# Nystrom attention and a multiplicative FFN on one core: the opening reordered, the second batch's attention moved, the iterated inverse on eight tiles

## The chip, the cores and the metric

The kernel runs on one core of one Trainium2 chip. A core has five engines: TensorE (PE in the profile; its weight loads are PEld), VectorE (DVE), ScalarE (ACT), GpSimd (POOL) and SyncE (SP). Each works through its own queue in order and they wait for one another by semaphores. Transfers are issued from the queues of SP, ACT and POOL and carried out by 16 DMA engines. Matmul results go to PSUM, everything else lives in SBUF.

The metric is the device time of one execution in microseconds. The profile is one execution taken by the hardware profiler; its span runs from the first to the last instruction.

## The reference

The inputs are q, k and v of 8 batches, 8 heads, 576 positions and 64 columns, and four weights. Everything is FP32 in and out.

```python
q_lm = q.reshape(B, H, m, S // m, D).mean(axis=3)      # m = 32 landmarks of 18 rows
k_lm = k.reshape(B, H, m, S // m, D).mean(axis=3)
A  = sm(q, k_lm);  Bm = sm(q_lm, k_lm);  C = sm(q_lm, k)     # softmax of scaled products
Z = Bm.transpose(0, 1, 3, 2) / (norm1(Bm) * norminf(Bm) + 1e-06)
for _ in range(6):
    Z = 2 * Z - Z @ Bm @ Z
x = A @ Z @ C @ v                                      # heads put side by side: 4608 x 512
a = x @ w1;  b = x @ w2                                # 512 x 1024 each
out = (a * b) @ w3 @ w_out                             # 1024 x 1024, 1024 x 512
```

`Z` is an inverse of the 32 x 32 matrix `Bm` by iteration, one for each batch and head.

## The kernel before, in words

**Fold.** `w3 @ w_out` doesn't depend on the tokens, so it is multiplied out once into `w34` (1024 x 512, FP16). For precision both factors are split into a high and a low FP16 half and three of the four cross products are summed. `turn(j, cc)` transposes half a row block of w3 on PE (four FP32 transposes into a `big` PSUM buffer, L453), ACT copies the high half out (L458) and DVE makes the low half (L459). `split_wout` does the same to w_out in four pieces on DVE (L444, L446). A fold step is the three matmuls of 512 columns for one j and one c (L488); there are 8 row blocks j of 8 steps c, so 64 steps. When a row block is done, ACT copies it out (L491).

**Attention.** `attention` is a generator that a batch passes through in 18 steps: the landmarks' matmul (L162) and `lm`; `Bm` (L178); the scores of C (L203) in two steps; scores of A (L253) in two; C @ v (L281, L286) in two; six steps of the inverse (L344); two that normalise A (L329), and four blocks of `g` (L390), the last of the two being in one step with the first block. `g` is `Z C v` times w1 or w2, in blocks of 128 x 1024. The eight heads of a batch lie as 4 x 2: head h of four on partitions 32h to 32h+31, and qd in 0, 1 on the columns.

In the inverse, `sz_` holds 96 columns per qd: 32 of the matrix that is squared (the identity is added to it) and 64 of the vectors that it is applied to. One iteration multiplies the 32 x 32 matrix with all 96 columns, on the four diagonal 32 x 32 tiles of the array, qd by qd; DVE copies the new matrix (L350) and adds the 64 columns to the old ones (L351). The last iteration leaves the matrix out.

**Before attention.** `load_qk` fetches k and q of a batch with a cast to FP16, on POOL's queue. `transposes` turns them by DMA transposes on SP's queue (L89), four to a batch. `landmarks` sums groups of 18 rows and splits the sum in two FP16 halves on POOL, in six instructions each for k and q (L145 to L154).

**Up and down.** For each batch `up(st, j, w)` multiplies A's normalised scores with a 128-column block of g (L404): w = 0 gives a, copied out by ACT (L408), w = 1 gives b, and DVE multiplies both into `ab` (L410). `down` multiplies `ab` with `w34` (L424) for 128 rows at a time in two halves; ACT copies out (L430) and SP stores.

**Order.** The program is written in the order in which it is issued, and each engine keeps it: there is no planner. While batch b goes through `up` and `down`, batch b + 2's loads and landmarks and batch b + 1's attention are woven in by `steps`. The first batch's attention is woven into the fold. PSUM has eight banks: three `big` buffers of two banks, one `small`, one `acc`. SBUF pools have two buffers for most tiles; w3 blocks have three, w_out has one whole tile.

The opening of the program, before:

```python
        nc.gpsimd.tensor_copy(out=gate, in_=wof[:, 2, 0:1])    # holds q and k back until w_out's 2nd piece
        load_qk(sts[0], 0)
        load_w3(2)
        ...
        steps(fd, 5)
        load_w3(3)
        turn_all(0)
        load_v(sts[0], 0)
        steps(fd, 8)
```

Of the kernel before, what the change touches and what calls it, by code (L numbers as in the profile page):

```python
# [14 lines left out]
H = 8  # L15
# [16 lines left out]
def kernel(  # L32
# [52 lines left out]
    def transposes(st, t, hs):  # L85
        if "qkT" not in st:
# [6 lines left out]

    ident = consts.tile([128, 128], FP32, name="ident")
    nc.gpsimd.memset(ident, 0.0)
    nc.gpsimd.affine_select(out=ident, in_=ident, compare_op=ALU.not_equal, fill=1.0,
                            base=0, pattern=[[-1, 128]], channel_multiplier=1)

    def constants():

        mask4 = consts.tile([128, 4, 32], FP32, name="mask4")
        par = consts.tile([128, 2], FP32, name="par")
        ones = consts.tile([128, 1], FP32, name="ones")
        eye = consts.tile([128, 2, 32], FP32, name="eye")
        iit = consts.tile([128, 2, 64], FP16, name="iit")
        onesq = consts.tile([128, 2, 4, 2, 4], FP16, name="onesq")
        nc.vector.memset(mask4, 0.0)
        nc.vector.memset(par, 0.0)
        nc.vector.memset(ones, 1.0)
        nc.vector.memset(onesq, 0.0)  # L110
        for i in range(2):
            sl = slice(64 * i, 64 * i + 64)
            nc.vector.memset(par[sl, i:i + 1], 1.0)
            for jj in range(2):
                nc.vector.tensor_copy(out=iit[sl, jj, :], in_=ident[sl, sl])
        for h in range(4):
            sl = slice(32 * h, 32 * h + 32)
            nc.vector.memset(mask4[sl, h, :], 1.0)
            for qd in range(2):
                nc.vector.tensor_copy(out=eye[sl, qd, :], in_=ident[sl, sl])  # L120
                nc.vector.memset(onesq[sl, qd, :, qd, h:h + 1], 1.0 / X64)

        selc = consts.tile([128, 2, 4, 128], FP16, name="selc")
        lomask = consts.tile([128, 1], FP32, name="lomask")
        selr = consts.tile([128, 8], FP32, name="selr")
        nc.vector.memset(selc, 0.0)
        nc.vector.tensor_tensor(out=selr, in0=eye[:, 0, 0:8], in1=eye[:, 0, 8:16], op=ALU.add)
        nc.vector.reduce_sum(out=lomask, in_=eye[:, 0, 8:16], axis=AX.X)
        nc.vector.tensor_scalar(out=lomask, in0=lomask, scalar1=-1.0, scalar2=None, op0=ALU.mult)
        for c in range(4):  # L130
            sl = slice(32 * c, 32 * c + 32)
            for qd in range(2):
                nc.vector.tensor_copy(
                    out=selc[sl, qd, c, :].rearrange("p (h m) -> p h m", m=32),
                    in_=selr[sl, 4 * qd:4 * qd + 4].unsqueeze(2).to_broadcast([32, 4, 32]),
                )
        return mask4, par, ones, eye, iit, onesq, selc, lomask


    def landmarks(st, t):  # L140
        if "parts" not in st:
            st["parts"] = pz.tile([128, 2, 2, H, 32], FP16, name="parts")
        x = st["qkT"][:, t, :, :, :]
        tr = pat.tile([128, H, NP], FP32, name="tr", bufs=1)
        nc.gpsimd.tensor_tensor(out=tr, in0=x[:, :, 0, :], in1=x[:, :, 1, :], op=ALU.add)  # L145
        nc.gpsimd.tensor_tensor(out=tr, in0=tr, in1=x[:, :, 2, :], op=ALU.add)  # L146
        t3 = tr.rearrange("p h (l g) -> p h l g", g=3)
        o = pat.tile([128, H, 32], FP32, name="o3", bufs=1)
        hi, lo = st["parts"][:, 0, t, :, :], st["parts"][:, 1, t, :, :]
        nc.gpsimd.tensor_tensor(out=o, in0=t3[:, :, :, 0], in1=t3[:, :, :, 1], op=ALU.add)  # L150
        nc.gpsimd.tensor_tensor(out=o, in0=o, in1=t3[:, :, :, 2], op=ALU.add)  # L151

        nc.gpsimd.tensor_copy(out=hi, in_=o)
        nc.gpsimd.tensor_tensor(out=lo, in0=o, in1=hi, op=ALU.subtract)  # L154


    def attention(st, bank=None):
# [111 lines left out]
        sz_ = pz.tile([128, 2, 96], FP32, name="sz_")  # L269
        for qd in range(2):  # L270
            nc.vector.scalar_tensor_tensor(
                out=sz_[:, qd, 0:32], in0=psR[:, 32 * qd:32 * qd + 32], scalar=nrn[:, qd:qd + 1],
                in1=eye[:, qd, :], op0=ALU.mult, op1=ALU.add)
# [63 lines left out]
        for it in range(6):  # L337
            last = it == 5
            psI = small()
            o = 32 if last else 0  # L340
            for qd in range(2):
                for h in range(4):
                    sl = slice(32 * h, 32 * h + 32)
                    nc.tensor.matmul(psI[sl, 96 * qd + o:96 * qd + 96], sz_[sl, qd, 0:32],  # L344
                                     sz_[sl, qd, o:96], start=True, stop=True,
                                     tile_position=(32 * h, 32 * h))
            pv_ = psI[:, 0:192].rearrange("p (a m) -> p a m", m=96)
            if not last:
                nsz = pz.tile([128, 2, 96], FP32, name="sz_")
                nc.vector.tensor_copy(out=nsz[:, :, 0:32], in_=pv_[:, :, 0:32])  # L350
                nc.vector.tensor_tensor(out=nsz[:, :, 32:96], in0=sz_[:, :, 32:96],  # L351
                                        in1=pv_[:, :, 32:96], op=ALU.add)
                sz_ = nsz
            else:
                xd = pz.tile([128, 2, 64], FP32, name="xd")
                nc.vector.tensor_tensor(out=xd, in0=sz_[:, :, 32:96], in1=pv_[:, :, 32:96],
                                        op=ALU.add)
# [84 lines left out]
    def split_wout(wof, c0):  # L442
        sl = slice(c0, c0 + 2)
        nc.vector.tensor_scalar(out=wsp[:, 0, sl, :], in0=wof[:, sl, :], scalar1=WS, scalar2=None,  # L444
                                op0=ALU.mult)
        nc.vector.scalar_tensor_tensor(out=wsp[:, 1, sl, :], in0=wof[:, sl, :], scalar=WS,  # L446
                                       in1=wsp[:, 0, sl, :], op0=ALU.mult, op1=ALU.subtract)

    def fold(pf, wof, w3f):
        def turn(j, cc):  # L450
# [5 lines left out]
            w3t = pf.tile([128, 2, 4, 128], FP16, name="w3t")  # L456
# [4 lines left out]
            return w3t  # L461


        blocks = [(0, 0), (1, 0), (0, 1), (1, 1)] + [(j, cc) for j in range(2, 8) for cc in range(2)]
        turned, psW = {}, {}

        def turn_next(n):
            if n < 16:
                turned[blocks[n]] = turn(*blocks[n])

        turn_next(0)
        split_wout(wof, 0)
        for n, (j, cc) in enumerate(blocks):
            if cc == 0:
                psW[j] = small() if j in (1, 3) else acc()
            for c4 in range(4):
                c = 4 * cc + c4

                if n < 4 and c4 == 1:
                    turn_next(n + 1)  # L480
                    if n < 3:
                        split_wout(wof, 2 * n + 2)
                elif n >= 4 and cc == 0 and c4 == 0:
                    turn_next(n + 1)
                elif n >= 4 and cc == 1 and c4 == 1:
                    turn_next(n + 1)
                for a, b in ((0, 0), (0, 1), (1, 0)):
                    nc.tensor.matmul(psW[j][:, :], turned[j, cc][:, a, c4, :], wsp[:, b, c, :],  # L488
                                     start=(c == 0 and a + b == 0), stop=(c == 7 and a == 1))
                if c == 7:  # L490
                    nc.scalar.activation(out=w34[:, j, :], in_=psW[j][:, :], func=AXF.Copy,  # L491
                                         scale=1.0 / (WS * WS))
                yield
# [14 lines left out]
    with tc.tile_pool(name="pf", bufs=2) as pf:  # L508
        wof, w3f = pf.tile([128, 8, DM], FP32, name="wof", bufs=1), {}
# [8 lines left out]
        for j, cc in ((0, 0), (1, 0), (0, 1), (1, 1)):  # L518
            load_w3(j, cc)
        for c in range(0, 8, 2):  # L520
            nc.scalar.dma_start(
                out=wof[:, c:c + 2, :],
                in_=moe_w_out[128 * c:128 * c + 256, :].rearrange("(c p) f -> p c f", p=128))
# [4 lines left out]
        for _ in range(8):  # L528
            nc.tensor.matmul(psw[:, 0, :], warm[:, 0:128], warm, start=True, stop=True)

        nc.gpsimd.tensor_copy(out=gate, in_=wof[:, 2, 0:1])
        load_qk(sts[0], 0)
        load_w3(2)
        mask4, par, ones, eye, iit, onesq, selc, lomask = constants()
        fd = fold(pf, wof, w3f)
        steps(fd, 5)
        load_w3(3)
        turn_all(0)
        load_v(sts[0], 0)
        steps(fd, 8)  # L540
        load_w3(4)
        landmarks(sts[0], 1)
        load_weight(0, moe_w1)
        landmarks(sts[0], 0)
        load_weight(1, moe_w2)
        load_qk(sts[1], 1)
        steps(fd, 8)
        load_w3(5)
        steps(fd, 8)
        load_w3(6)  # L550
        steps(fd, 6)
        at = attention(sts[0])
        for n in range(28):
            steps(at)
            if n == 4:
# [3 lines left out]
            if n == 10:  # L559
                landmarks(sts[1], 1)  # L560
                landmarks(sts[1], 0)
                load_qk(sts[2], 2)
            steps(fd)
        steps(at, 30)
        steps(fd, 64)
    pab = ctx.enter_context(tc.tile_pool(name="pab", bufs=3))
    at = attention(sts[1], acc)
    steps(at)


    for b in range(B):
# [10 lines left out]
        for j in range(8):  # L582
            up(st, j, 0)
            steps(at)
# [46 lines left out]
```

## Time and profile before

| | |
|---|---|
| median of 5 runs | 304.4 us (301.79 to 305.02) |
| the profiled execution | 305.99 us, span 304.2 us |
| PE busy | 281.4 us, 93% of the span |
| DVE, POOL, ACT busy | 162.8, 147.0, 121.6 us |
| first matmul of the fold | 9.42 us |
| the sixteen steps of row blocks 0 and 1 done | 31.40 us |
| the second batch's landmark matmul, first up after it | 85.12 us, 85.55 us |
| from there to the third batch's landmark matmul | 27.76 us |

A page shows one execution. Its first part gives the busy time of each engine; the second cuts the span in 40 slices, with a digit for the busy tenths of each engine in each slice, the clock granted to PE in tenths (PEclk), and the busy share of the DMA engines. A timeline gives groups of instructions in order of time: start, duration, engine, line, operation, out<-in, partitions and shape, count, and in brackets how long the engine was idle before and what ended that. Matmul ends are modelled, so the distance between starts of groups is the better measure of what a group holds PE.

### The profile page before, as it was taken

What the parts mean: (1) busy time and instruction counts of PE and PEld (TensorE: products, weight loads), DVE (VectorE), ACT (ScalarE), POOL (GpSimd) and SP (SyncE); (2) the same over time, 40 slices, a digit from 0 to 9 for tenths busy, and PEclk for the clock granted to TensorE, in tenths of its full rate; (3) what the DMA queues carried; (4) which work ended last, traced back from release to release, by engine and by line L of the source; (5) the groups of instructions that cost most, each with busy time, mean ns of one, the idle gap of its engine ahead of it and who ended that gap; (6) DMA issues with size and microseconds to landing.
All of it is one profiled execution on the core that took longest, in us unless ns stands there. A gap on an engine that the chain in (4) does not pass through costs nothing.

```text
span 304.2 us, 9351 instructions
## 1 busy us (share of the span) xinstructions
PE 281.4 (93%) x3976; PEld 154.8 (51%) x3976; DVE 162.8 (54%) x411; ACT 121.6 (40%) x197; POOL 147.0 (48%) x187
## 2 busy tenths in 40 slices
PE   5586999599999999999999999999999999999994
PEld 2233555343566437643764674367447544754641
DVE  6533224246355657664665765476566556666620
ACT  1102235104255257235733752474167235624532
POOL 0205964109629925980796299239907930600000
PEclk9579999989999999999999999999999999999998
DMA  7989999992299939993999599389959632003114
GB/s 230 327 158 190 274 225 250 213 134 42 33 208 210 207 83 167 193 211 91 149 210 226 123 203 213 99 115 163 246 152 168 134 104 74 2 18 90 38 45 127
DMA packets 66121, 46.74 MB, mean 154 GB/s; under 512 B 39712, under 2 KB 58144, under 8 KB 66080
## 3 DMA queue, kind: packets, MB, share of 16 engines
q1 hardware_dynamic: 51360, 32.52, 50.0%
q0 software_dynamic: 13632, 11.54, 24.4%
q10 hardware_dynamic: 1088, 2.10, 1.9%
q8 instruction: 31, 0.51, 0.7%
q14 instruction: 10, 0.08, 0.1%
HBM read 38.80 MB, written 9.44 MB: 159 GB/s over the span
## 4 chain that ended last, share of the span: by engine, by line
PE 85%; ACT 6%; DVE 4%; issue 2%; DMA 2%; ACTq 0%
PE big L404 20%; PE acc L424 12%; PE acc L488 11%; PE big L424 10%; PE small L344 7%; PE big L390 6%; PE small L488 3%; PE small L281 2%; ACT a_sb L408 2%; PE big L453 2%; PE acc L281 2%; DMA wof<-in_moe_w_out_dram 2%; DVE wsp L446 2%; PE big L329 2%; PE big L203 2%
## 5 line engine op out<-in xcount | busy, mean ns | idle before, releaser
L404 PE MATMUL big<-ahat,gt 128*128 128x288 f16 x512 | 74.5, 287 | 2.2 <-ACT a_sb L408 1.6
L410 DVE TENSOR_TENSOR ab<-a_sb,big 128x576 f16<-128x576 f16 x64 | 48.0, 751 | 18.1 <-PE big L404 10.8
L408 ACT CAST a_sb<-big 128x576 f16<-128x576 f32 x64 | 40.9, 639 | 39.1 <-PE big L404 38.4
L404 PEld LDWEIGHTS <-gt 128*128 128x128 f16 x512 | 46.1, 98 | 18.7 <-issue 4.4
L214 POOL TENSOR_TENSOR t<-ect 96x384 f32<-96x384 f32 x16 | 15.9, 995 | 71.6 <-ACT ect L207 71.1
L488 PE MATMUL acc<-wsp,w3t 128*128 128x512 f16 x144 | 39.8, 405 | 9.3 <-DVE wsp L444 5.9
L424 PE MATMUL acc<-w,ab 128*128 128x512 f16 (+1 forms) x192 | 40.9, 382 | 0.0
L145 POOL TENSOR_TENSOR tr<-qkT 128x768 f32<-128x768 f16 x16 | 27.2, 1702 | 28.0 <-DMA qkT<-qkn 28.0
L424 PEld LDWEIGHTS <-ab 128*128 128x128 f16 (+1 forms) x320 | 24.1, 100 | 32.2 <-issue 9.7
L488 PEld LDWEIGHTS <-w3t 128*128 128x128 f16 x192 | 18.3, 101 | 31.6 <-issue 14.2
L424 PE MATMUL big<-w,ab 128*128 128x512 f16 x128 | 32.8, 382 | 0.0
L396 DVE TENSOR_SCALAR gt<-big 128x1024 f16<-128x1024 f32 x16 | 19.6, 1225 | 20.2 <-PE big L390 20.2
L459 DVE SCALAR_TENSOR_TENSOR w3t<-big,w3t 128x512 f16<-128x512 f32 x16 | 11.1, 692 | 29.7 <-ACT w3t L458 29.6
L146 POOL TENSOR_TENSOR tr<-tr,qkT 128x768 f32<-128x768 f32 x16 | 26.3, 1641 | 1.3
L430 ACT ACTIVATE o_sb<-acc 128x512 f32<-128x512 f32 x20 | 11.9, 597 | 36.1 <-PE acc L424 35.1
L458 ACT ACTIVATE w3t<-big 128x512 f16<-128x512 f32 x16 | 9.5, 595 | 35.7 <-PE big L453 35.7
L394 ACT ACTIVATE gt<-big 128x1024 f16<-128x1024 f32 x16 | 16.4, 1024 | 7.9 <-PE big L390 7.9
L390 PE MATMUL big<-wup,zt 64*32 64x512 f16 x512 | 19.2, 381 | 0.0
L430 ACT ACTIVATE o_sb<-big 128x512 f32<-128x512 f32 x16 | 9.6, 597 | 23.3 <-PE big L424 23.3
L207 ACT ACTIVATE ect<-big 96x768 f32<-96x768 f32 x16 | 12.9, 806 | 2.3 <-PE big L203 1.9
L151 POOL TENSOR_TENSOR o<-o,tr 128x256 f32<-128x256 f32 x16 | 12.8, 800 | 1.3
L332 DVE TENSOR_TENSOR ahat<-eat,big 128x576 f16<-128x576 f16 x16 | 12.0, 748 | 1.4 <-PE big L329 1.4
(298 smaller groups left out, 354.5 us busy)
## 6 DMA issues: line engine op xcount, KB each, us to landing
vt<-in_v_dram SPq DMA_DIRECT2D x8, 1152.0 KB, 9.3
qkn<-in_k_dram POOLq DMA_DIRECT2D x8, 576.0 KB, 9.7
qkn<-in_q_dram POOLq DMA_DIRECT2D x8, 576.0 KB, 12.7
out_dram<-o_sb SPq DMA_DIRECT2D x24, 192.0 KB, 2.3
w3f<-in_moe_w_dram SPq DMA_DIRECT2D x6, 512.0 KB, 8.2
out_dram<-o_sb SPq DMA_DIRECT2D x24, 128.0 KB, 3.1
wof<-in_moe_w_out_dram ACTq DMA_DIRECT2D x4, 512.0 KB, 8.3
wup<-in_moe_w_dram POOLq DMA_DIRECT2D x4, 512.0 KB, 10.6
```

The lines of the kernel that those rows point to most:

```text
L145: nc.gpsimd.tensor_tensor(out=tr, in0=x[:, :, 0, :], in1=x[:, :, 1, :], op=ALU.add)
L146: nc.gpsimd.tensor_tensor(out=tr, in0=tr, in1=x[:, :, 2, :], op=ALU.add)
L344: nc.tensor.matmul(psI[sl, 96 * qd + o:96 * qd + 96], sz_[sl, qd, 0:32], sz_[sl, qd, o:96], start=True, stop=True, tile_position=(32 * h, ...
L390: nc.tensor.matmul(psG[32 * h:32 * h + 32, qd, :], zt[rs, i, h, :], wup[rs, h, w, fs], start=(i == 0), stop=(i == 1), tile_position=(64 * ...
L394: nc.scalar.activation(out=g[:, :, w, fs], in_=psG, func=AXF.Copy, scale=1.0 / ZS)
L396: nc.vector.tensor_scalar(out=g[:, :, w, fs], in0=psG, scalar1=1.0 / ZS, scalar2=None, op0=ALU.mult)
L404: nc.tensor.matmul(p[:, c, 0:HS], st["g"][:, qd, w, 128 * j:128 * j + 128], st["ahat"][qd][:, c, :], start=(qd == 0), stop=(qd == 1))
L408: nc.scalar.copy(out=st["a_sb"], in_=p[:, :, 0:HS])
L410: nc.vector.tensor_tensor(out=st["ab"][:, j, :].rearrange("p (c s) -> p c s", c=2), in0=st["a_sb"], in1=p[:, :, 0:HS], op=ALU.mult)
L424: nc.tensor.matmul(pso[o:o + sz, :], ab[:, j, s0:s0 + sz], w34[:, j, :], start=(j == 0), stop=(j == 7), tile_position=(0, o))
L430: nc.scalar.activation(out=o_sb, in_=pso[:, :], func=AXF.Copy, scale=1.0 / (X64 * X64))
L488: nc.tensor.matmul(psW[j][:, :], turned[j, cc][:, a, c4, :], wsp[:, b, c, :], start=(c == 0 and a + b == 0), stop=(c == 7 and a == 1))
```

## The change

**q and k of the first batch on PE.** `turn_on_pe` makes 12 transposes of 96 x 128 FP16 blocks into a `big` buffer, for four heads of k or q, and ACT or DVE copies them to `qkT`. Four calls take the place of the four DMA transposes of this batch. The first batch's landmarks of k stay on POOL, those of q go to DVE, in two halves.

**Fold.** w_out is held in pieces of 256 rows, three buffers; three are loaded by ACT's queue, the fourth by SP's once the first is split. The order of steps weaves row blocks 0 and 1 by piece: both take the two steps of piece 0, then both of piece 1, and so on. w3's transposed halves have four buffers. Warm-up matmuls are ten instead of eight.

**Loads.** w1 and w2 are issued right behind the first batch's q and k; v moves ahead of w3 blocks 3 and 4; the second batch's q and k come earlier. The first batch's attention starts after 24 fold steps (35 before), with two fold steps between its steps instead of one.

**Second batch's attention.** It no longer starts ahead of the first batch's `up`, but after j = 2, and takes 0, 0, 0, 1, 1, 1, 2, 2 steps in the eight j. Its k landmarks come after the fold on POOL, its q landmarks on DVE at j = 1.

**Inverse.** The matrix of the product is kept apart with 2I added (`tz_`), so that the product gives the new 96 columns outright. The order is h outside, qd inside, and qd = 1 goes to the tile beside the diagonal (`t = h ^ qd`): eight tiles with one product each. The two heads' places swap at each of the six iterations. The result goes to a `big` buffer, one bank for each qd.

```diff
+    def turn_on_pe(st, t, h0, copy):
+        if "qkT" not in st:
+            st["qkT"] = pat.tile([128, 2, H, 3, NP], FP16, name="qkT")
+        ps = psp.tile([128, 2, 1024], FP16, name="big", bufs=3)
+        for i in range(2):
+            for n in range(6):
+                nc.tensor.transpose(
+                    out=ps[:, i, NP * n:NP * n + NP],
+                    in_=st["qkn"][0:NP, t, h0 + 2 * i + n // 3, 128 * (n % 3):128 * (n % 3) + 128],
+                    identity=ident16[0:NP, 0:NP])
+        copy(out=st["qkT"][:, t, h0:h0 + 4, :, :].rearrange("p (i h) c s -> p i (h c s)", i=2),
+             in_=ps[:, :, 0:6 * NP])
...
-    def landmarks(st, t):
+    def landmarks(st, t, eng=nc.gpsimd):
...
+        for h0 in ((0,) if eng is nc.gpsimd else (0, 4)):
+            own, n = ("", H) if eng is nc.gpsimd else ("v", 4)
...
+            eng.tensor_tensor(out=tr, in0=x[:, :, 0, :], in1=x[:, :, 1, :], op=ALU.add)
...
         for it in range(6):
             last = it == 5
-            psI = small()
+            psI = big()
             o = 32 if last else 0
-            for qd in range(2):
-                for h in range(4):
+            for h in range(4):
+                for qd in range(2):
                     sl = slice(32 * h, 32 * h + 32)
-                    nc.tensor.matmul(psI[sl, 96 * qd + o:96 * qd + 96], sz_[sl, qd, 0:32],
+                    t = h ^ qd
+                    nc.tensor.matmul(psI[32 * t:32 * t + 32, qd, o:96], tz_[sl, qd, :],
                                      sz_[sl, qd, o:96], start=True, stop=True,
-                                     tile_position=(32 * h, 32 * h))
-            pv_ = psI[:, 0:192].rearrange("p (a m) -> p a m", m=96)
+                                     tile_position=(32 * h, 32 * t))
             if not last:
-                nsz = pz.tile([128, 2, 96], FP32, name="sz_")
-                nc.vector.tensor_copy(out=nsz[:, :, 0:32], in_=pv_[:, :, 0:32])
-                nc.vector.tensor_tensor(out=nsz[:, :, 32:96], in0=sz_[:, :, 32:96],
-                                        in1=pv_[:, :, 32:96], op=ALU.add)
-                sz_ = nsz
+                tz_ = pz.tile([128, 2, 32], FP32, name="tz_")
+                nc.vector.tensor_tensor(out=tz_, in0=psI[:, :, 0:32], in1=eye2, op=ALU.add)
+                sz_ = pz.tile([128, 2, 96], FP32, name="sz_")
+                nc.vector.tensor_copy(out=sz_, in_=psI[:, :, 0:96])
...
+        before = {0: [(turn, 0, 0), (split, 0), (turn, 1, 0), (split, 1)],
+                  2: [(turn, 0, 1)], 3: [(split, 2)], 6: [(turn, 1, 1)], 7: [(split, 3)],
+                  14: [(turn, 2, 0)]}
+        order = [(j, 2 * i + c) for i in range(4) for j in range(2) for c in range(2)]
+        for j in range(2, 8):
+            before[8 * j] = [(turn, j, 1)]
+            before[8 * j + 5] = [(turn, j + 1, 0)] if j < 7 else []
+            order += [(j, c) for c in range(8)]
...
-        nc.gpsimd.tensor_copy(out=gate, in_=wof[:, 2, 0:1])
+        nc.gpsimd.tensor_copy(out=gate, in_=wof[1][:, 0, 0:1])
         load_qk(sts[0], 0)
+        load_weight(0, moe_w1)
+        load_weight(1, moe_w2)
+        mask4, par, ones, eye2, iit, onesq, selc, lomask = constants()
+        fd = fold(pf, wof, w3f, wsp)
+        steps(fd, 1)
+        load_wout(3, nc.sync)
         load_w3(2)
-        mask4, par, ones, eye, iit, onesq, selc, lomask = constants()
-        fd = fold(pf, wof, w3f)
-        steps(fd, 5)
+        load_v(sts[0], 0)
+        steps(fd, 11)
         load_w3(3)
-        turn_all(0)
-        load_v(sts[0], 0)
-        steps(fd, 8)
+        steps(fd, 1)
+        turn_on_pe(sts[0], 1, 0, nc.scalar.copy)
+        turn_on_pe(sts[0], 1, 4, nc.vector.tensor_copy)
+        landmarks(sts[0], 1)
+        load_qk(sts[1], 1)
+        steps(fd, 4)
         load_w3(4)
-        landmarks(sts[0], 1)
-        load_weight(0, moe_w1)
-        landmarks(sts[0], 0)
-        load_weight(1, moe_w2)
-        load_qk(sts[1], 1)
-        steps(fd, 8)
...
+        turn_on_pe(sts[0], 0, 0, nc.scalar.copy)
+        turn_on_pe(sts[0], 0, 4, nc.vector.tensor_copy)
+        landmarks(sts[0], 0, nc.vector)
+        steps(fd, 7)
         at = attention(sts[0])
-        for n in range(28):
+        for n in range(20):
             steps(at)
-            if n == 4:
+            if n == 1:
+                load_w3(5)
+            elif n == 5:
+                load_w3(6)
+            elif n == 9:
                 load_w3(7)
                 load_v(sts[1], 1)
                 turn_all(1)
-            if n == 10:
-                landmarks(sts[1], 1)
-                landmarks(sts[1], 0)
-                load_qk(sts[2], 2)
-            steps(fd)
-        steps(at, 30)
+            steps(fd, 2)
         steps(fd, 64)
+        landmarks(sts[1], 1)
+        load_qk(sts[2], 2)
     pab = ctx.enter_context(tc.tile_pool(name="pab", bufs=3))
     at = attention(sts[1], acc)
-    steps(at)
...
         for j in range(8):
             up(st, j, 0)
-            steps(at)
+            if b == 0 and j == 1:
+                landmarks(sts[1], 0, nc.vector)
+            steps(at, (0, 0, 0, 1, 1, 1, 2, 2)[j] if b == 0 else 1)
             up(st, j, 1)
```

## The prediction

> **What bounds the kernel now.** I read the page's busy shares first, then its 40 slices, then TensorE's (PE's) own timeline, slice by slice, and last what the queues did in the slices where PE stood still.
>
> ```profile
> PE 281.4 (93%) x3976; PEld 154.8 (51%) x3976; DVE 162.8 (54%) x411; ACT 121.6 (40%) x197; POOL 147.0 (48%) x187
> ...
> PE   5586999599999999999999999999999999999994
> ...
> PEclk9579999989999999999999999999999999999998
> DMA  7989999992299939993999599389959632003114
> ```
>
> PE is the bound from slice 5 on (a slice is 7.6 us), with one hole at slice 8; what it lacks is in the first four slices, where the clock was also lowered. There the transfers are nearly full. So a microsecond of PE work is worth a microsecond after 31 us, and before that it is the order of arrivals and of DVE's work that counts. PE's timeline of the opening (start, duration, group, idle before and its releaser):
>
> ```profile
> 4.69 0.97 PE L453 MATMUL big<-ident,w3f 128*128 128x128 f32 x4
> 9.42 0.58 PE L488 MATMUL acc<-wsp,w3t 128*128 128x512 f16 x1 [3.76 <-DVE wsp L444]
> ...
> 15.82 2.29 PE L488 MATMUL acc<-wsp,w3t 128*128 128x512 f16 x5 [0.68 <-DVE wsp L446]
> ...
> 26.04 0.38 PE L488 MATMUL acc<-wsp,w3t 128*128 128x512 f16 x1 [1.36 <-DVE wsp L444]
> ...
> 31.84 3.40 PE L488 MATMUL acc<-wsp,w3t 128*128 128x512 f16 x15
> ...
> 59.07 0.25 PE L281 MATMUL small<-vt,ect 96*32 96x64 f32 x2 [3.58 <-issue]
> ```
>
> Two things are lost here. PE waits for DVE's splits of w_out (L444, L446), in pieces; and after the first 3.76 us of idling the products run at 458 ns (2.29 us for 5) instead of 215 (3.24 us for 15 in the chain of waits). The woven products of row blocks 0 and 1 (48 matmuls of 215 ns, 10.3 us) therefore take from 9.42 to 31.40. The hole at 55.5 us is 3.58 us inside one group, for which the profile names no releaser.
>
> The inverse, in the steady part:
>
> ```profile
> 124.63 0.53 PE L344 MATMUL small<-sz__1616 32*32 32x96 f32 x16
> 125.09 1.15 PE L404 MATMUL big<-ahat,gt 128*128 128x288 f16 x8
> ...
> 132.77 0.43 PE L344 MATMUL small<-sz__1877 32*32 32x64 f32 x16
> 133.13 1.04 PE L424 MATMUL acc<-w,ab 128*128 128x512 f16 x4
> ```
>
> From start to the next group's start an iteration holds PE 0.46 us, the last (64 columns) 0.36. The 16 matmuls of 32 columns at L267 take 0.25. That is a straight line: 0.145 us and 0.105 us per 32 columns.
>
> **What the Trainium skill says.** "TensorE: Matmul & The Clock Gate", Part 1: PE runs at half clock after about 3.4 us without work; the trace agrees (3.76 us idle, then 458 ns). The same page, Part 3: matmuls on separate tiles of the array run together, for one matmul's time and about 4 ns a tile; the trace doesn't contradict it, but shows no 32x32 tile off the diagonal. "TensorEngine Tiling (Array Packing)", Gotcha 1: different row tiles cannot access one PSUM bank at once; here four row tiles write one bank and still overlap (two rounds, not eight, fit the line above). "DMA: Bandwidth & Descriptors", Queues, rings and completion order: each DMA engine takes turns between queues, packet by packet. I use it for the landing of k and q.
>
> **The opening, step by step.** *First product.* ACT issues three w_out transfers, not four. The fourth was the one that started at 5.75 and kept the table load until 6.15. PE warms up with 10 matmuls of 0.449 us, so the first turn ends at about 6.3; ACT's copy (0.60), DVE's low half (0.69) and split (0.69, then 1.23) end at about 9.6, against 10.6 before. The idle gap is then cut in two (6.7 to 8.4, 8.9 to 9.6), so I take full clock.
>
> *The 16 woven steps.* DVE needs 4 x 0.69 + 4 x 1.92 = 10.4 us from 7.0, so to 17.4; PE needs 10.3 + 2 x 0.44 (the other two turns lie earlier) = 11.2 us from 9.6, so to about 20.9. PE is the later one. Before: 31.4. Gain 10.5. The fourth piece of w_out now waits on SP for a free buffer (9.6 us); at the 5.0 to 10.3 us that w_out took to land it is there at 15 to 20, wanted at 15.4: up to 2 us lost on DVE, of which I take 0.5.
>
> *k and q on PE.* 48 transposes, not in the trace. The nearest row, L203 (96 rows, 64 columns), is 44 ns apiece; L453's FP32 ones are 109. So 2.1 to 5.2 us; I take 60 ns, 2.9 us, all on the path. The four copies out (1152 columns; rows of 1024 take 1.02 on ACT, 1.23 on DVE) lie beside products. With them go four DMA transposes and 6.97 us of SP's time, which the PE doesn't feel now except through later w3 loads.
>
> *Moved loads.* PE is in order, so everything of the fold queues behind the k turn (wanted near 19 us) and the q turn (near 25). k and q are issued on POOL at 9.1 as before, when they alone took until 18.3; now v, a w_out piece and three w3 blocks are in SP's queue beside them, and w1 and w2 behind them on POOL's. With turns between the queues k (half of 5.8 us of transfer, doubled, from 11.4) lands near 17 and q near 23: 2 us to spare each. That is cover, not certainty. w3 block 3 lands at about 27, wanted at 28.
>
> *k's landmarks on POOL, q's on DVE.* POOL's set takes 5.9 us (26.2 to 33.2 the first time). On DVE, by the row of 512 columns (688 ns), 384 columns are 0.53 and 128 about 0.27: 2 x (2 x 0.53 + 4 x 0.27) = 4.3 us in DVE's queue, with the low half of w3 block 3 behind it; PE may wait 1 us at the first attention step. I take 1.
>
> *The rest of fold and first attention.* Before, 31.40 to 85.12 = 53.7 us, the same PE work in both. Two fold steps to each attention step give more cover; of the 3.58 us hole and the slow clock after it (61 to 63 us: 0.65 us more on three products and more behind) I take 2 us as gone. So the first up starts after 20.9 + 0.5 + 2.9 + 53.7 + 1 - 2 = 77.0 instead of 85.1: 8.1. Bounds: 12.5 (the hole gone, cheap transposes), 4 (late loads).
>
> **The second batch's attention.** PE's work is only moved. Two costs. q's landmarks, 4.3 us by the sum above, stand in DVE's queue before the copy of up(1, 1). PE can go on through up(3, 0), about 2 us, then the landmark product waits, and the evictions behind it: 2.3 us. And with 16 steps placed in this batch of 18, g's last two blocks come with no down between them. A block is 0.56 us on PE but 1.02 on ACT or 1.23 on DVE to evict, and the next batch's lm copy queues behind one on ACT: 1.5 us. Together +3.8 (bounds 1.5 and 6).
>
> **The inverse.** Two products to a tile become one, so the slope halves: 0.145 + 0.16 + 4 more tiles at 4 ns = 0.32 instead of 0.46, and 0.27 instead of 0.36. 8 x (5 x 0.14 + 0.09) = 6.3 us. DVE's additions (2I added on the copy, 192 columns copied instead of 64, next to L350 at 230 ns and L351 at 280) are about 0.1 us an iteration on an engine at 54%, hidden by the 0.97 us of down beside them. The result now takes one of three `big` buffers, which the two evictions of up also need; in the two iterations inside the up loop that leaves an eviction of 0.75 us against 0.8 to 0.95 us of other PE work: at most 0.1 us each, 1 us in all. I take 5.5 (bounds 8 and 0; the off-diagonal tiles can't be bounded by a row, see below).
>
> **The sum.** 8.1 - 3.8 + 5.5 = 9.8 us off the profiled execution's 306.0 (span 304.2 and 1.8 around it): 296. That execution was 1.6 above the median of the runs, so 304.4 - 9.8 = 294.6; since more of my doubtful terms were taken dear than cheap (the hole, 1 us of waits), I round to 294.
>
> **Rivals.** *Late loads.* If SP's queue gets more than its turn, k lands after 24 and q after 27; PE stands at the k turn for over 3.4 us and restarts at half clock. It loses 5 us more and ends at about 299. For: DMA share is over 1.0 between 8 and 18 us already. Against: SP's first pieces are 0.5 MB each.
> *The inverse gains nothing* (the 16 matmuls are limited by issue, not by their columns): 304.4 - 4.3 = 300. For: L281 issues 48 in 0.69 us, 14 ns each, so 16 need 0.23. Against: the slope over 32, 64 and 96 columns.
> *Slower.* Two column tiles of one row group can't stream together in the 32x32 shape. The order is now h outside, so each second matmul waits for the first and holds all behind: 5 x 0.16 + 0.145 = 0.95 us instead of 0.46, 0.68 instead of 0.36, 8 x (5 x 0.49 + 0.32) = 22 us; 304.4 - 4.3 + 22 = 322. It decides from 4.3 / 48 = 0.09 us more per iteration. Against: L281 (96x32) and L390 (64x32) hold several column tiles of the same rows and do overlap (0.56 us for 16 matmuls of 512 columns that would need 3.4 in turn).
>
> **Chances.** Forecast 0.62, late loads 0.14, no gain in the inverse 0.10, slower 0.07, and 0.07 for more than I count (all bounds at their good end: 304.4 - 12.5 + 1.5 - 8 = 285). The range goes from 286 to 301. A change of under 1%, 3 us, can't be told from none here: faster 0.88, same 0.05, slower 0.07.
>
> **What would show it.** Right: the first turn of k near 19 us with no wait on its load, PE busy without a gap from 9.6, the clock line full in slice 2, the first up near 77, inverse groups 0.3 to 0.33 us apart from the next group. Wrong: PE waiting on qkn or w3 loads; the first products still at 458 ns; inverse groups of 0.46 or more; up groups behind an eviction in every batch.

## The result, and the profile after

The changed kernel takes 301.33 us in the median (299.16 to 302.50, 22 runs), the kernel before 304.50 (41 runs). Some executions fall in a slower state with a lower granted clock (six of the 41 before, from 306.4 us up), so ratios and gains, here and below, are taken from the others, whose median before is 303.72. The ratio is 0.9911, 95% interval 0.9890 to 0.9931. So it gained 2.4 us, where 9.8 were forecast. The profiled execution took 300.44 us, span 298.5.

The page after: the summary of engines, then from the 40 slices (7.5 us each) the rows of TensorE (PE), its clock and the DMA engines.

```profile
PE 275.6 (92%) x4026; PEld 151.4 (51%) x4026; DVE 177.9 (60%) x454; ACT 124.2 (42%) x199; POOL 135.2 (45%) x176
...
PE   6866999999869989999999999999999999999993
...
PEclk9998999999999999999999999999999999999999
DMA  6999998939921939975996899379949632012124
```

PE has 5.8 us less to do and the first two slices are fuller, but the third and fourth (15 to 30 us) are at 6 (8 and 6 before), and there is a new dent in the eleventh and twelfth (75 to 90 us), where there was none before. PE's timeline shows what stands in both: start, duration, group, and in brackets the idle time before with its releaser.

```profile
7.76 0.38 PE L490 MATMUL acc<-wsp,w3t 128*128 128x512 f16 x1 [0.72 <-DVE wsp L469]
9.02 1.24 PE L490 MATMUL acc<-wsp,w3t 128*128 128x512 f16 x5 [0.88 <-DVE wsp L471]
...
17.44 0.81 PE L490 MATMUL acc<-wsp,w3t 128*128 128x512 f16 x3
20.89 1.40 PE L100 MATMUL big<-ident,qkn 96*128 96x96 f16 x24 [2.64 <-DMA qkn<-in_k_dram]
22.09 1.48 PE L490 MATMUL acc<-wsp,w3t 128*128 128x512 f16 x3
...
29.72 1.19 PE L100 MATMUL big<-ident,qkn 96*128 96x96 f16 x24 [2.50 <-DMA qkn<-in_q_dram]
...
77.39 3.36 PE L426 MATMUL big<-ahat,gt 128*128 128x288 f16 x24
84.05 0.71 PE L183 MATMUL small<-parts,iit 128*128 128x512 f16 x2 [2.41 <-DVE parts L174]
85.03 1.38 PE L426 MATMUL big<-ahat,gt 128*128 128x288 f16 x8 [0.27 <-DVE ab L432]
...
105.43 0.62 PE L412 MATMUL big<-wup,zt 64*32 64x512 f16 x16 [0.76 <-DVE ahat L356]
...
106.95 1.49 PE L412 MATMUL big<-wup,zt 64*32 64x512 f16 x48
108.37 0.61 PE L183 MATMUL small<-parts,iit 128*128 128x512 f16 x2
```

The splits of w_out (L469, L471) hold PE only twice more, at the start. Thirteen of the sixteen woven steps are done at about 18.1 us; the other three come behind k's turn, from 22.09 to 25.5 us. Before, all sixteen were done at 31.4. PE stands before k's turn (2.64 us) and q's (2.50 us), and after the first runs at half clock (the three products at 22.09 take 1.27 us to the next group's start, 0.65 at full clock). The second batch's landmark product (L183 at 84.05) comes 6.66 us after the first `up` and waits 2.41 us for DVE. Where it went, by the landmark products' starts (L162 before, L183 after):

| stretch | before | after |
|---|---|---|
| to the first `up` | 85.55 | 77.39 |
| first `up` to the third batch's landmarks | 27.33 | 30.98 |
| third batch's landmarks to the end | 191.3 | 190.1 |

The first row looks as forecast (77.0). It isn't, as the experiments show: the profiled execution before was itself late there. In the second row 3.65 us are given back.

The inverse, in a later batch, by the same view; two groups in the `up` loop and two in the `down` loop:

```profile
120.27 0.40 PE L369 MATMUL big<-sz__1709,tz__1710 32*32 32x96 f32 x16
120.67 1.14 PE L426 MATMUL big<-ahat,gt 128*128 128x288 f16 x8
121.74 0.40 PE L369 MATMUL big<-sz__1851,tz__1849 32*32 32x96 f32 x16
122.23 0.31 PE L331 MATMUL big<-eat,onesq 128*32 128x144 f16 x8
...
124.10 0.39 PE L369 MATMUL big<-sz__1877,tz__1875 32*32 32x96 f32 x16
124.42 1.05 PE L446 MATMUL acc<-w,ab 128*64 128x512 f16 x8
```

In the `down` loop an iteration holds PE 0.32 us (0.46 before), as forecast. In the `up` loop it holds 0.49 (121.74 to 122.23), more than before; the group at 120.27 shows 0.40 here, and 0.49 in a later batch. DVE's timeline beside it shows why:

```profile
119.86 0.75 DVE L432 TENSOR_TENSOR ab<-a_sb,big 128x576 f16<-128x576 f16 x1
...
121.43 0.75 DVE L432 TENSOR_TENSOR ab<-a_sb,big 128x576 f16<-128x576 f16 x1 [0.17 <-PE big L426]
```

The evictions of `up` end at 120.61 and 122.18; PE's next groups, which need a `big` buffer, start 0.06 and 0.05 us later.

### The profile page after: what moved, and what is told of

It is laid out like the page before. It is cut to its first block, busy times and chain, and to the rows that moved or that the text cites. A ratio compares the mean times of both kernels' runs of the same rounds, so it can differ in the third digit from the quotient of the medians.

```text
span 298.5 us, 9452 instructions
## 1 busy us (share of the span) xinstructions
PE 275.6 (92%) x4026; PEld 151.4 (51%) x4026; DVE 177.9 (60%) x454; ACT 124.2 (42%) x199; POOL 135.2 (45%) x176
## 4 chain that ended last, share of the span: by engine, by line
PE 73%; DMA 9%; DVE 8%; ACT 6%; issue 2%; POOL 0%; ACTq 0%; DVEq 0%
PE big L426 16%; PE acc L446 13%; PE big L446 10%; PE acc L490 9%; DMA qkn<-in_q_dram 7%; PE big L412 6%; DVE ab L432 4%; PE big L369 4%; ACT a_sb L430 3%; DMA wof<-in_moe_w_out_dram 2%; PE small L305 2%; PE acc L305 2%; PE big L477 2%; PE big L353 1%; PE big L224 1%
## 5 line engine op out<-in xcount | busy, mean ns | idle before, releaser
L426 PEld LDWEIGHTS <-gt 128*128 128x128 f16 x512 | 47.2, 98 | 20.6 <-issue 6.1
L490 PE MATMUL acc<-wsp,w3t 128*128 128x512 f16 x168 | 42.1, 384 | 1.6 <-DVE wsp L471 0.9
L166 POOL TENSOR_TENSOR tr<-qkT 128x768 f32<-128x768 f16 x14 | 23.0, 1641 | 20.4 <-DMA qkT<-qkn 10.8
L418 DVE TENSOR_SCALAR gt<-big 128x1024 f16<-128x1024 f32 x16 | 19.5, 1224 | 17.7 <-PE big L412 17.7
L167 POOL TENSOR_TENSOR tr<-tr,qkT 128x768 f32<-128x768 f32 x14 | 23.0, 1641 | 1.1
L482 ACT ACTIVATE w3t<-big 128x512 f16<-128x512 f32 x16 | 9.5, 597 | 19.9 <-PE big L477 19.5
L172 POOL TENSOR_TENSOR o<-o,tr 128x256 f32<-128x256 f32 x14 | 11.2, 799 | 1.1
```

Of the source, the lines that this page charges most:

```text
L166: eng.tensor_tensor(out=tr, in0=x[:, :, 0, :], in1=x[:, :, 1, :], op=ALU.add)
L167: eng.tensor_tensor(out=tr, in0=tr, in1=x[:, :, 2, :], op=ALU.add)
L418: nc.vector.tensor_scalar(out=g[:, :, w, fs], in0=psG, scalar1=1.0 / ZS, scalar2=None, op0=ALU.mult)
L426: nc.tensor.matmul(p[:, c, 0:HS], st["g"][:, qd, w, 128 * j:128 * j + 128], st["ahat"][qd][:, c, :], start=(qd == 0), stop=(qd == 1))
L490: nc.tensor.matmul(psW[j][:, :], turned[j, c // 4][:, a, c % 4, :], wsp[:, b, c, :], start=(c == 0 and a + b == 0), stop=(c == 7 and a == 1))
```

## The experiments

Medians are of six runs where no other number is given, each beside runs of the kernel before on the same chip (303.90 us for the first four kernels, 303.68 for the next four, 303.46 for the last). A gain is the distance from that median; a ratio is to the same runs.

**The inverse alone.** The kernel before with the changed inverse and nothing else.

```diff
-            psI = small()
+            psI = big()
...
+                    t = h ^ qd
-                                     tile_position=(32 * h, 32 * h))
+                                     tile_position=(32 * h, 32 * t))
```

> The kernel before with the new inverse alone. Theory (the two iterations that share the up loop lose their gain to the wait for a big buffer): 0.75 us from the first batch, 0.40 from each of the other seven, 3.6 us off, 300.9. Rival (all 48 iterations gain 0.13, as the prediction had it, and the opening's trace only hides it by chance stalls): 5.5 to 6 us off, 298.7. The traces are to show groups of the inverse 0.33 us apart in the down part and 0.45 to 0.5 in the up part.

Measured: 300.07 us (299.39 to 301.36), ratio 0.9883 (0.9852 to 0.9914): a gain of 3.8 (2.6 to 4.5 by the interval), as the theory has it and not the rival's 5.5. From one batch's landmarks to the next it is 26.66 and 28.68 us instead of 27.07 and 29.06: 0.40 a batch. Its groups hold PE as in the changed kernel:

```profile
121.03 0.39 PE L350 MATMUL big<-sz__1634,tz__1635 32*32 32x96 f32 x16
121.52 1.14 PE L407 MATMUL big<-ahat,gt 128*128 128x288 f16 x8
122.59 0.39 PE L350 MATMUL big<-sz__1776,tz__1774 32*32 32x96 f32 x16
123.09 0.31 PE L312 MATMUL big<-eat,onesq 128*32 128x144 f16 x8
```

0.49 and 0.50 us in `up`. Four iterations in `down` save 3 x 0.13 + 0.08 = 0.47, the two in `up` lose 0.07: 0.40.

This run has the opening of before, and serves as a second look at it. Its hole in the fold is there too (3.02 us at 54 to 57). But its first landmark product starts at 44.43 instead of 45.88, and the second batch's at 82.52 instead of 85.12. Between the two lies the first batch's inverse, 0.7 us cheaper at most. So some 2 us of the opening that I measured from was that one execution's. Where they lie can be seen: in the kernel before the products ran at half clock until about 19 us (2.29 us for the five at 15.82), here only until about 14:

```profile
15.95 1.24 PE L491 MATMUL acc<-wsp,w3t 128*128 128x512 f16 x5 [0.88 <-DVE wsp L449]
```

The sixteen woven steps are done at 29.94 here (31.40), which is 1.5 of the 2 us; the shorter hole is 0.6.

**What holds k and q up.** Two edits to the changed kernel, each taking away other transfers until q has landed. In the first, w3's block 3 waits on SP, and v behind it. In the second, w1 and w2 wait on POOL, behind q in the same queue.

```diff
-        load_v(sts[0], 0)
+        w3f[3] = pf.tile([128, DF], FP32, name="w3f", bufs=3)
+        nc.gpsimd.tensor_copy(out=w3f[3][0:NP, 0:1], in_=sts[0]["qkn"][0:NP, 0, 7, 0:1])
         load_w3(3)
+        load_v(sts[0], 0)
```

> The changed kernel with w3 block 3 held back on SP's queue until q of the first batch has landed, and v issued behind it. Theory (v and w3 on SP's queue take most of the turns that k and q need): k lands by 17 and q by 21 us instead of 20.9 and 29.7, PE's waits of 2.6 and 2.5 us at the turns of k and q go, and the half clock behind them: 4 to 6 us off, 296 to 297. Rival (w1 and w2 behind them on POOL's queue are the cause, or the transfers are simply full): waits as before, 301 or later.

```diff
         load_qk(sts[0], 0)
+        nc.gpsimd.tensor_copy(out=gate2, in_=sts[0]["qkn"][:NP, 0, 7, 0:1])
         load_weight(0, moe_w1)
         load_weight(1, moe_w2)
```

> The changed kernel with w1 and w2 held back on POOL's queue until q of the first batch has landed, SP's queue as it was. Theory (SP's queue is the cause): k and q land as before, the same two waits, 301.3 within 1 us. Rival (w1 and w2 are the cause): the waits go, 4 to 6 us off.

Measured: 302.16 us (16 runs, ratio 0.9946, 0.9928 to 0.9965) with w3 and v held, 306.66 (ratio 1.0102, 1.0059 to 1.0145) with w1 and w2 held. PE's timeline with w3 and v held:

```profile
20.51 1.19 PE L100 MATMUL big<-ident,qkn 96*128 96x96 f16 x24
...
25.00 1.19 PE L100 MATMUL big<-ident,qkn 96*128 96x96 f16 x24
...
32.50 0.71 PE L183 MATMUL small<-parts,iit 128*128 128x512 f16 x2 [0.93 <-DVE parts L174]
...
39.94 0.66 PE L477 MATMUL big<-ident,w3f 128*128 128x128 f32 x4 [2.27 <-DMA w3f<-in_moe_w_dram]
```

Neither turn waits, and the first attention starts 3.7 us earlier. k and q land at 18.2 and 21.1 us (20.9 and 29.7 in the changed kernel). Then w3 block 4, behind v in the queue, is late by 2.27 us, PE runs at half clock behind this wait, and the gain is gone: the median is 5 to 6 us above the theory. With w1 and w2 held:

```profile
20.67 1.19 PE L100 MATMUL big<-ident,qkn 96*128 96x96 f16 x24 [0.85 <-DMA qkn<-in_k_dram]
28.50 1.61 PE L100 MATMUL big<-ident,qkn 96*128 96x96 f16 x24 [3.18 <-DMA qkn<-in_q_dram]
39.60 1.03 PE L183 MATMUL small<-parts,iit 128*128 128x512 f16 x2 [3.26 <-DVE parts L174]
```

k and q land nearly as late as ever (20.7 and 28.5). The time is over 5 us above the theory's for another reason: POOL, which stands at the gate, does k's landmarks only from 31.1 to 38.0 us, beside DVE's of q. In the changed kernel DVE does its own alone, in 4.9 us (31.62 to 36.48); here they take 9.0 (30.82 to 39.87), and one addition of 128 x 128 (L171) takes 1.65 us beside POOL and 0.33 once POOL is done. So the transfers on SP's queue slow k and q, and what lies behind them on their own queue by no more than the runs differ among themselves (with the opening alone, below, nothing is held and q lands at 28.7). This agrees with the Trainium skill, "DMA: Bandwidth & Descriptors", Queues, rings and completion order, by which each DMA engine takes turns between the queues: a transfer shares with those in other queues and not with those behind it in its own.

**The second batch's attention at its old place.** The changed kernel, but with both landmarks of the second batch on POOL, the first step ahead of the first `up`, and a step for each j.

```diff
+        landmarks(sts[1], 0)
...
+    steps(at)
...
-            if b == 0 and j == 1:
-                landmarks(sts[1], 0, nc.vector)
-            steps(at, (0, 0, 0, 1, 1, 1, 2, 2)[j] if b == 0 else 1)
+            steps(at)
```

> The changed kernel with the second batch's attention as in the kernel before: both landmarks on POOL, its first step ahead of the first up, one step to each j. Theory (moving it cost 4 us: landmarks of q on DVE, two blocks of g without cover): the stretch from the first up to the third batch's landmarks falls from 31.0 us to 27.0, 297.5. Rival (PE's work is only moved, the stretch is as long because the opening ended early and its transfers come late): the first up waits for the second batch's transposes or landmarks, 300 or more.

Measured: 295.10 us (294.63 to 296.47), ratio 0.9720 (0.9689 to 0.9751). The move had cost 6.2 us (5.8 by the ratios), more than I had forecast for it (3.8). From the first `up` to the third batch's landmarks it is 26.24 us instead of 30.98, so 4.7 of them lie there by these two executions:

```profile
77.57 0.59 PE L183 MATMUL small<-parts,iit 128*128 128x512 f16 x2
78.00 0.65 PE L426 MATMUL big<-ahat,gt 128*128 128x288 f16 x4
...
104.24 0.61 PE L183 MATMUL small<-parts,iit 128*128 128x512 f16 x2
```

**The move parted in two.** The changed kernel with the second batch's q landmarks on POOL; the attention stays late.

```diff
+        landmarks(sts[1], 0)
...
-            if b == 0 and j == 1:
-                landmarks(sts[1], 0, nc.vector)
```

> The changed kernel with one edit: q's landmarks of the second batch on POOL after the fold instead of on DVE at j = 1; the second batch's attention stays late (0, 0, 0, 1, 1, 1, 2, 2 steps). It parts the 6.2 us that the move cost. Theory (prediction's two terms, 2.3 us for landmarks on DVE and the rest for g blocks that come three together without cover): 301.3 - 2.3 = 299, the wait of 2.41 us at the second batch's landmark product gone. Rival (the late place alone costs it all, the wait for DVE only takes the place of another): 301.3, within 0.7 us.

Measured: 296.36 us (295.12 to 299.44), ratio 0.9775 (0.9714 to 0.9835). That is lower than the theory (299) and the rival (301.3). By the medians DVE's landmarks cost 5.0 of the 6.2 us, and the late place 1.3; the interval of this run is 1.8 us to each side, so 1.3 alone can't be told from none. PE's timeline:

```profile
77.47 3.86 PE L426 MATMUL big<-ahat,gt 128*128 128x288 f16 x28
81.16 0.59 PE L183 MATMUL small<-parts,iit 128*128 128x512 f16 x2
...
104.54 0.86 PE L183 MATMUL small<-parts,iit 128*128 128x512 f16 x2
```

The landmark product comes 3.69 us after the first `up` (6.66 in the changed kernel), and the third batch's 23.38 us later (24.32). From the first `up` to the third batch's landmarks it is 27.07 us, against 26.24 at the old place. These 0.83 us are the late place, and 0.76 of them stand in one wait, which both kernels with it show (105.43 above): the two steps that normalise A come together, and the first block of `g` waits for a buffer that DVE still reads for `ahat`. The three blocks of `g` behind each other hold PE 1.42 us (106.95 to 108.37), not more than when spread.

DVE's timeline of the changed kernel has the two losses from the landmarks:

```profile
78.81 0.75 DVE L432 TENSOR_TENSOR ab<-a_sb,big 128x576 f16<-128x576 f16 x1 [3.95 <-ACT a_sb L430]
79.48 0.55 DVE L166 TENSOR_TENSOR trv<-qkT 128x384 f32<-128x384 f16 x1
...
84.23 1.41 DVE L432 TENSOR_TENSOR ab<-a_sb,big 128x576 f16<-128x576 f16 x2
```

For 4.8 us (79.48 to 84.23) no result of `up` is multiplied out. PE goes on through up(3, 0) and stands at the landmark product, which needs these landmarks; then two evictions come together, and the `up` groups that follow wait for them in turn (0.27 us at 85.03, and groups of 1.38 us for 1.14). By these two executions it is 3.9 us, by the medians 5.0 and by the ratios 4.1; the difference is within the spread of the runs.

**The opening alone.** The changed opening with the old inverse and the second batch at its old place.

```diff
         for it in range(6):
-            psI = big()
+            psI = small()
...
-                    t = h ^ qd
-                                     tile_position=(32 * h, 32 * t))
+                                     tile_position=(32 * h, 32 * h))
```

> The opening of the change alone: q and k on TensorE, w_out in pieces, the woven row blocks, the moved loads; the inverse and the second batch's attention as before. Theory (the three parts add up): inverse alone gave 3.9 us, so 295.1 + 3.9 = 299.0, that is 5 us under before, with the first up near 78 and the third batch's landmark product 27 us after it. Rival (opening and inverse share a gain, such as the hole in the fold that the inverse's step fills): 297 or less.

Measured: 299.17 us (297.99 to 301.71), ratio 0.9864 (0.9811 to 0.9917): a gain of 4.5 (2.5 to 5.7 by the interval), although the first `up` starts at 77.54. The parts add up as the theory has it, within these intervals: 4.5 + 3.8 = 8.3, and with both of them the gain was 8.8.

About 1 us is lost far behind the opening. From the fifth batch's landmarks to the sixth's it is 30.42 us instead of 29.06, and PE stands inside a group of the inverse:

```profile
178.78 0.52 PE L363 MATMUL small<-sz__2998 32*32 32x96 f32 x12 [1.01 <-issue]
```

All nine kernels with the new opening have such a hole there (0.53 to 1.29 us); the kernel before and the one with the inverse alone don't, and have the hole in the fold instead. For neither does the profile name a releaser. In all fourteen holes of this kind (over 0.25 us, after 30 us, in the eleven traces) PE goes on 1.3 to 1.7 us after a transfer of the queue that the page calls `instruction` (q8) has ended, 16 KB each and about 30 in an execution. This suggests that PE waits for the next piece of its program; no run tests it.

**k and q without the waits.** As with the old place above, and w3's block 3 held as in the hold of w3 and v, but v now last.

```diff
-        load_v(sts[0], 0)
+        w3f[3] = pf.tile([128, DF], FP32, name="w3f", bufs=3)
+        nc.gpsimd.tensor_copy(out=w3f[3][0:NP, 0:1], in_=sts[0]["qkn"][0:NP, 0, 7, 0:1])
         load_w3(3)
...
         load_w3(4)
+        load_v(sts[0], 0)
```

> Second batch's attention at its old place, and w3's block 3 held until q has landed, with v behind w3's blocks 3 and 4 (so v is late, not w3). Theory (k's and q's waits of 2.64 and 2.50 us are what the opening lost, and v has some 17 us to spare): both waits go, PE doesn't wait for w3 in their place, the first landmark product starts near 32.5 instead of 36.5, first up near 74.5: 291.5. Rival (the transfers are full to 44 us, so what is freed here is missed further on): PE waits for a w3 block or v by about as much, first up near 78: 295.

Measured: 291.48 us (290.49 to 292.43), ratio 0.9604 (0.9558 to 0.9650). PE's timeline:

```profile
19.73 1.19 PE L100 MATMUL big<-ident,qkn 96*128 96x96 f16 x24
...
24.22 1.19 PE L100 MATMUL big<-ident,qkn 96*128 96x96 f16 x24
...
28.55 0.63 PE L477 MATMUL big<-ident,w3f 128*128 128x128 f32 x4 [0.56 <-POOL parts L175]
...
31.71 0.72 PE L183 MATMUL small<-parts,iit 128*128 128x512 f16 x2 [0.59 <-DVE parts L174]
```

The first attention starts at 31.71 instead of 36.52, and the first `up` at 73.33 instead of 78.00. Short waits of 0.56 and 0.59 us are left. The waits cost 3.6 us in the median (3.5 by the ratios), and weren't forced by full transfers: v can wait, since nothing reads it before 42 us.

**The inverse's two groups in `up`.** The old place again, and in these two iterations the two results go to the two single-bank buffers, `small` and `acc`, instead of a `big` one. DVE takes them out with four small instructions instead of two.

```diff
-            psI = big()
+            psI = big() if it not in own else None
+            pI = [psI[:, 0], psI[:, 1]] if it not in own else [small(), acc()]
```

> The second batch's attention is back at its old place, as in the run before, and the two iterations of the inverse that lie in the up loop write their two results to the single-bank buffers instead of a big one; DVE makes four small instructions instead of two in these. Theory (the 0.49 us that these two groups hold PE, against 0.33 in the down part, is the wait for a big buffer, on both sides): the two groups fall to about 0.33 us, 0.3 us a batch, 2 us in all: 293 against 295.1. Rival (the time there is DVE's own, its queue between up's evictions): the groups stay at 0.45 to 0.5 us or the product behind them waits, 295 or a little more.

Measured: 293.94 us (293.16 to 296.93), ratio 0.9695 (0.9642 to 0.9749). The median lies between the two theories, and the runs overlap those with `big` (294.63 to 296.47). The timeline decides. The sixteen records of a group are listed one by one here; the first is shown, and the group behind:

```profile
87.63 0.27 PE L370 MATMUL small<-sz__1155,tz__1156 32*32 32x96 f32 x1
...
87.96 1.15 PE L433 MATMUL big<-ahat,gt 128*128 128x288 f16 x8
89.04 0.27 PE L370 MATMUL small<-sz__1297,tz__1296 32*32 32x96 f32 x1
...
89.36 0.31 PE L331 MATMUL big<-eat,onesq 128*32 128x144 f16 x8
```

0.33 and 0.32 us instead of 0.50 and 0.49, and nothing waits behind. From the third batch's landmarks to the end it is 188.1 us instead of 189.8: 1.7. The median gained only 1.2; in the stretch before, this execution has a hole of 1.08 us (to 93.18), of the kind above, that the other doesn't have.

**All three repairs.** Old place, v last, single-bank buffers: the three edits above in one kernel.

```diff
-    at = attention(sts[1], acc)
+    at = attention(sts[1], acc, (0, 1))
+    steps(at)
...
+        w3f[3] = pf.tile([128, DF], FP32, name="w3f", bufs=3)
...
         load_w3(4)
+        load_v(sts[0], 0)
```

> The three repairs together: second batch's attention at its old place, w3's block 3 held until q has landed with v behind w3's blocks 3 and 4, and the inverse's two iterations in the up loop in single-bank buffers. Theory (the held loads and the buffers act in different stretches, so they add): 291.5 - 1.2 = 290.3, or 289.5 if the buffers are worth the 2 us that the distance between groups says. Rival (part of the single-bank run's 1.2 us was its luckier opening, 76.22 instead of 78.00 to the first up): 291.5, no difference.

Measured: 289.55 us (288.25 to 291.31), ratio 0.9544 (0.9502 to 0.9586): 11.8 us under the changed kernel. It came out at the good end of the theory. In this execution PE's clock is full from the start, and behind the first products the one long wait left in the opening is for w3 (1.68 us at 28.04).

## Why the prediction was wrong

The sum was 8.1 - 3.8 + 5.5 = 9.8; the runs give 4.5 - 6.2 + 3.8 = 2.1, with 2.4 measured. All three terms were off to the same side. The sign was right, and so were the mechanisms, but for the uncovered g blocks; the sizes failed.

**Opening, 8.1 forecast, 4.5 measured.** The step that failed is "2 us to spare each" for k and q. k landed at 20.9 us instead of 17 and q at 29.7 instead of 23. Turns between the queues were right; what was doubled was too small. POOL's queue (q0) and SP's (q1), from 14.5 to 20 us and from 20 to 30 us, in packets, MB and share of the DMA engines' time:

```profile
q1 hardware_dynamic: 581, 0.97, 61.2%
q0 software_dynamic: 621, 0.47, 55.2%
...
q0 software_dynamic: 970, 1.17, 67.3%
q1 hardware_dynamic: 544, 1.41, 46.8%
```

So SP's queue doesn't get more than its turn in time, only in bytes. But I had given k and q 2.9 us each alone. In the kernel before, where SP's queue is empty beside them, their first bytes come at 12.2 us, k lands at 16.7 and q at 19.5: 4.5 and 7.3 us. Doubled, from the first bytes at 11.8 in the changed kernel, that makes 20.8 for k and 26.4 for q (an estimate from these times). That fits k; why q was 3.3 us later still stays open. That the hold of v and w3's block 3 takes the waits away shows that it is these loads, though not which of the two. The waits cost 3.6 us by the run without them; the opening would have gained 8.1 then. I had the two waits as a rival ("late loads", 299 us), with 5 us for them: they came, as a part of the sum and not in its place, and without its reason, that SP's queue gets more than its turn. The rival also wanted over 3.4 us of standing for the half clock; 2.64 us were enough here, while behind 2.50 us at q's turn the clock was full.

That the first `up` came at 77.39 with 77.0 forecast is no confirmation. The 3.58 us hole and the half clock behind it, 5.2 us together, went whole where I took 2, and the 48 transposes held PE 2.2 us (1.20 and 1.03), not 2.9. By the starts, some 11.4 us were won in the woven steps (nine products more at 0.22 us from 18.1 on make 20.0 us without k's turn; 20.9 were forecast, 31.4 before), 5.2 at the hole, and 1.2 because the first batch's inverse is shorter and the second's landmark product no longer stands ahead of the first `up`. Lost were 5.1 us in the waits, 1.5 at half clock after the first, 2.2 in the turns and 0.3 at the landmark product: 8.7 together, where the starts of the first `up` lie 8.2 apart. And the base was wrong: about 2 us of the opening was particular to the profiled execution, as the run with the inverse alone shows, and I took the whole gain off the median. I had corrected the span for the 1.6 us above the median, not the stretch where they lay. Without these 2 us, the 1.2 that belong to the other parts and the 1 lost near 178 us, 4.0 of the 8.2 are left, near the 4.5 measured.

Full clock for the first products wasn't sure either. In five of the nine kernels with this opening the five products that start between 9.2 and 9.8 us take 2.25 to 2.29 us, in the other four, the changed kernel's trace among them, 1.24.

**Second batch, +3.8 forecast, +6.2 measured.** The wait for landmarks on DVE was foreseen, with its place. Its size failed: "4.3 us in DVE's queue ... 2.3 us". The queue took 4.8, and I counted only the wait before the landmark product, not the evictions that come out of step behind it (0.9 us more in the trace). It is 5.0 us in the medians. The uncovered g blocks were put at 1.5, and the late place cost 1.3 in the medians and 0.8 in the traces; that this is near is luck, since it is the wait behind the two normalising steps and not the blocks.

**Inverse, 5.5 forecast, 3.8 measured.** An iteration's 0.32 us in `down` was right, and the last one's 0.27 nearly (0.28). The failed step is "at most 0.1 us each" for the `big` buffer. I had set an eviction's 0.75 us against the PE work between. From the timelines the eviction starts about 0.2 us after the product's end and its buffer is used 0.06 us after it, so 1.0 us stands against 0.54 us of `up` and 0.33 us of inverse: about 0.15 us lost in each, all that the iteration had gained. With single banks the loss is gone.

**Rivals.** The inverse does gain, so "gains nothing" falls, though its time (300) lies near the result. "Slower" falls: two column tiles of one row group do stream together. The range (286 to 301) just missed: it had no case in which all three terms are at their poor side at once.

## What to carry to other kernels

A load that is moved up is priced with every byte that shares the DMA engines until it is wanted, from all queues, and what has slack (here v) is put last. Before work goes to an engine because that engine is idle on average, look at what stands behind it in that queue: 4.8 us of landmarks ahead of evictions cost 4 to 5 us of the whole. And a gain that is read off one stretch of one execution is checked against a second execution of the same code before it is taken off a median.

## What the runs showed of the hardware

24 transposes of 96 x 128 in FP16 hold PE 1.03 us at full clock (29.72 to 30.75), 43 ns each. The Trainium skill, "TensorE: Matmul & The Clock Gate", Part 4, gives about 275 ns for one of 128 x 128 in a kernel, from its start to its end. One here is recorded with 206 ns, but the next starts 43 ns behind it; for a row of them that distance is the price.

Eight FP32 products on eight 32 x 32 tiles, two on each row group, four on each PSUM bank, start within 0.05 us of each other, a second set of eight 0.11 us behind, and all sixteen hold PE 0.32 us.

One addition of 128 x 128 on DVE takes 1.65 us while POOL does its landmarks, and 0.33 us after them, in the run that holds w1 and w2.
